# Squares and their seven block sums in one buffer, with one cast and one subtraction for the low parts

## The chip, the cores and the metric

The kernel runs on one core of one Trainium2 chip. The metric is the device time of one execution in microseconds (us); a run's number is the time of that one core. Five engines work in parallel, each through its own queue in order: TensorE (PE in the profile, its weight loads PEld), VectorE (DVE), ScalarE (ACT), GpSimd (POOL), and SyncE (SP), which issues the DMA transfers.

## What is computed

Two layers, of which the second stage takes nearly all of the matmuls. First a local attention (4 batches, 8 heads, 768 positions, head size 64): each position looks at keys less than 16 away and at one summary key for each block of 32. Its output `x` (3072 tokens, 512 wide) goes through a feed-forward layer with a squared ReLU:

```python
h = np.maximum(x @ w_in, 0.0)          # w_in  512 x 2048
return (h * h @ w_out)                 # w_out 2048 x 512
```

All products are made in float32 precision from two parts of each operand: a high part, rounded by a cast to `float32r`, and a low part, the rest. A product is high x high + high x low + low x high, so three matmuls.

## The kernel before

The 3072 tokens make 12 chunks of 256 (two tiles of 128). Chunks 0 and 1 and the preparation of the weights run in a start phase from a hand-written list of steps (`START`). From chunk 2 on, `period(c)` and `slot(c, n, ...)` write the program: a chunk has 8 slots, and slot n treats one pair p of blocks of 128 hidden units (256 hidden units in all). Every engine executes its instructions in the order in which the program writes them (the scheduler is off: `tc.manual_schedule`), so the order of the calls in `slot` is the order on each queue. A slot writes, in this order:

- the first layer of the pair: `ffn1_pair`, 24 matmuls of 256 columns (L392), into PSUM bank 4 or 5 (`ph`, alternating);
- in slot 7 the attention outputs of the next chunk's two tiles (`outputs`, L361), which read the transposed weights `pT`;
- the second layer of the pair of the slot before: `second`; in slots 0 and 3 also the scores of the next chunk's two tiles (L277);
- the lists `before`, the squares of this slot, `mid`, the rest of the squares, `after` and `last`. In them lies the next chunk's attention: maxima (`mask_max`, L304), exponentials (L312), sums' inverses (`inverse`, L322, L325), the norm on GpSimd (`norm`, L330), the 32x32 transposes (`turn`, L343), and the block sums of keys and values (L195, L200).

The second layer has two forms. The plain form (`second`, L586) is 12 matmuls of 512 columns. The other (`products`, L522) multiplies 2x2 blocks with seven block products instead of eight: 21 matmuls of 256 columns. It needs three sums of blocks of `w_out` (made once for each pair by `build(p, step)`: four steps on GpSimd, the fifth with casts on ScalarE, L499 and L500, and subtractions on VectorE, L501 and L502) and four sums of blocks of the squares, made in every slot. Before, chunks 0 to 2 are plain; from chunk 3 on all pairs but pair 0 use `products`. `BUILDS` says in which slot, and in which of the four lists (b, m, a, l), a step of a build stands: pairs 1 to 4 in chunk 2, the end of pair 4 and pairs 5, 7 and 6 in chunk 3. The sums of pairs 1, 3, 5 and 7 are stored to DRAM and loaded again in every chunk (`stream`).

The squares of a slot with `products`, before (`squares_and_sums`, `split_sums`): ScalarE makes `r` = ReLU (L400) and from `r` the high parts of three of the four blocks by Square (L406). VectorE overwrites `r` with the squares (L440) and makes the four sums in a second buffer `s`: two by one 256-wide subtraction (L443), two 128 wide (L448, L449). GpSimd subtracts the low parts of the three blocks, 384 wide (L447). After the list `mid`, ScalarE casts the sums (L453) and GpSimd subtracts their low parts, 512 wide (L454). A plain slot (`squares`) has ReLU and Square on ScalarE and the square and the low parts on VectorE (L411, L414).

Pieces that a sentence can't say:

```python
passes = [(m, n) for m in plain for n in range(3)] + [(m, n) for m in summed for n in range(2)]
for (blk, b, n_ps, o), n in passes + [(m, 2) for m in summed]:
    g_, w = ((gh_sb, 0), (gh_sb, 1), (gl_sb, 0))[n]      # n = 2 reads the low parts gl
```

The functions that the change touches, and what calls them:

Of the kernel before, what the change touches and what calls it, by code (L numbers as in the profile page):

```python
# [864 lines left out]
```

## Time and profile before

| | us |
|---|---|
| runs (three): median, lowest, highest | 667.4, 666.64, 669.68 |
| the profiled execution's own time | 667.81 |
| span of its profile | 666.0 |
| PE busy | 609.5 (92%), 5859 matmuls |
| VectorE (DVE) busy | 510.1 (77%) |
| ScalarE (ACT) busy | 291.6 (44%) |
| GpSimd (POOL) busy | 277.9 (42%) |
| chain that ended last, by engine | PE 39%, DVE 38%, ACT 12%, issue 5%, POOL 4%, DMA 1% |

The time of an execution and the span of its profile differ by what lies before the first and after the last instruction (1.8 us here). PE's busy time counts pipelined matmuls with modelled ends, so 92% does not say that PE has no time to lose. The start phase takes the span up to about 140 us, chunk 2 up to about 203 us, and chunks 3 to 11 the rest. In the views, an idle time in brackets, as `[2.15 <-DVE pT L343]`, stands behind the instruction that waited and names what came last; the line is that of the instruction that it waited for.

### The profile page before, as it was taken

Reading aid. Unit: us, or ns where it says so; the run is one execution under the profiler, and the core shown is the slowest. Engines: PE = TensorE matmul, PEld = TensorE weight load, DVE = VectorE, ACT = ScalarE, POOL = GpSimd, SP = SyncE. Lnnn points to the kernel's source line nnn. Section 1 sums busy time; section 2 is a strip of 40 time slices with the busy share of each in tenths; the row PEclk is TensorE's granted clock in tenths of the full one; section 3 lists DMA queues with packets and bytes.
Section 4 is the critical chain, followed back from the end, with each engine's and each line's share of the span. In section 5 each row is a group of like instructions: output and inputs, shape, how many; then the busy total and the mean of one; then the engine's idle time right before and its main releaser. Section 6 shows DMA issues by size and latency. Waiting matters only on the chain.

```text
span 666.0 us, 14839 instructions
## 1 busy us (share of the span) xinstructions
PE 609.5 (92%) x5859; PEld 567.6 (85%) x5859; DVE 510.1 (77%) x1240; ACT 291.6 (44%) x748; POOL 277.9 (42%) x252
## 2 busy tenths in 40 slices
PE   3689999999989788998999998998998999999997
PEld 2578888988878788998988998988998998998897
DVE  4898998957756876787787788788698588588554
ACT  3678685224444333443443443443434444443232
POOL 3635462005637662442453343343254244244242
PEclk9789999999989977999999999998999999999999
DMA  8689311550216421732621732732532432331410
GB/s 337 215 351 376 116 64 48 184 189 1 88 58 200 171 96 65 237 111 96 215 88 48 238 112 96 230 120 74 186 104 83 138 132 82 127 97 48 155 67 33
DMA packets 27638, 91.15 MB, mean 137 GB/s; under 512 B 3376, under 2 KB 3504, under 8 KB 25520
## 3 DMA queue, kind: packets, MB, share of 16 engines
q1 hardware_dynamic: 27568, 90.20, 39.2%
q8 instruction: 46, 0.75, 0.5%
q14 instruction: 24, 0.20, 0.1%
HBM read 80.75 MB, written 9.44 MB: 135 GB/s over the span
## 4 chain that ended last, share of the span: by engine, by line
PE 39%; DVE 38%; ACT 12%; issue 5%; POOL 4%; DMA 1%; DVEq 0%; SPq 0%; ACTq 0%; POOLq 0%
PE ph L392 17%; DVE pT L343 8%; DVE s L443 8%; PE zw L522 6%; ACT e_sb L312 5%; DVE r L440 4%; PE o_ps L463 4%; PE o_ps L522 4%; PE o_ps L586 3%; ACT r L400 2%; DVE s L448 2%; DVE s L449 2%; ACT gh L406 2%; DVE e_sb L304 2%; DVE w_sb L263 1%
## 5 line engine op out<-in xcount | busy, mean ns | idle before, releaser
L392 PE MATMUL ph<-xh,w_sb 128*128 128x256 f32 x1408 | 251.9, 281 | 2.0 <-DVE gl L414 1.1
L392 PEld LDWEIGHTS ph<-xh,w_sb 128*128 128x128 f32 x1408 | 215.9, 189 | 8.2 <-issue 2.7
L392 PE MATMUL ph<-xl,w_sb 128*128 128x256 f32 x704 | 197.1, 280 | 0.2
L392 PEld LDWEIGHTS ph<-xl,w_sb 128*128 128x128 f32 x704 | 132.8, 189 | 1.6 <-DVE xl L377 1.6
L447 POOL TENSOR_TENSOR gl<-r,gh 128x384 fp32r<-128x384 f32 x63 | 64.5, 1024 | 150.4 <-DVE r L440 145.7
L453 ACT CAST gh<-s 128x512 fp32r<-128x512 f32 x63 | 39.1, 621 | 181.2 <-DVE s L449 171.6
L454 POOL TENSOR_TENSOR gl<-s,gh 128x512 fp32r<-128x512 f32 x63 | 81.9, 1300 | 76.2 <-issue 58.4
L343 DVE STREAM_TRANSPOSE pT<-e_sb 32x256 f32<-32x256 f32 x228 | 99.4, 436 | 3.3
L400 ACT ACTIVATE r<-ph 128x512 f32<-128x512 f32 x85 | 50.3, 592 | 84.1 <-PE ph L392 36.7
L312 ACT ACTIVATE e_sb<-e_sb,nmx 128x120 f32<-128x120 f32 x192 | 73.5, 384 | 25.9 <-DVE nmx L304 25.9
L330 POOL TENSOR_TENSOR e_sb<-e_sb,sm 128x480 f32<-128x480 f32 x43 | 43.3, 1008 | 96.2 <-DVE sm L325 88.6
L443 DVE TENSOR_TENSOR s<-r 128x256 f32<-128x256 f32 x63 | 75.4, 1197 | 6.5
L440 DVE TENSOR_TENSOR r<-ph,r 128x512 f32<-128x512 f32 x63 | 43.5, 691 | 37.5 <-ACT gh L406 30.3
L406 ACT ACTIVATE gh<-r 128x384 fp32r<-128x384 f32 (+1 forms) x96 | 54.0, 562 | 20.5 <-PE o_ps L463 12.9
L522 PE MATMUL zw<-sums,gh 128*128 128x256 f32 x252 | 51.5, 286 | 0.7 <-ACT gh L453 0.6
L522 PE MATMUL zw<-w_sb,gh 128*128 128x256 f32 x252 | 51.7, 287 | 0.3 <-ACT gh L406 0.3
L522 PE MATMUL o_ps<-w_sb,gh 128*128 128x256 f32 x252 | 50.3, 281 | 0.0
L256 POOL TENSOR_TENSOR w_raw<-w_raw 128x1024 int32<-128x1024 int32 x16 | 34.2, 2147 | 37.0 <-DVE w_raw L251 13.9
L304 DVE CUSTOM_DVE_ANT_0 e_sb<-s_ps,mask_sb 128x120 f32<-128x120 f32 x192 | 42.6, 274 | 8.2 <-PE s_ps L292 5.8
L586 PE MATMUL o_ps<-w_sb,gh 128*128 128x512 f32 x144 | 46.1, 402 | 0.2 <-ACT gh L406 0.2
L411 DVE TENSOR_TENSOR ph<-ph,r 128x512 f32<-128x512 f32 x25 | 17.4, 695 | 33.6 <-ACT r L400 33.3
L522 PEld LDWEIGHTS zw<-sums,gh 128*128 128x128 f32 x252 | 39.5, 194 | 2.0 <-ACT gh L453 2.0
(119 smaller groups left out, 1165.4 us busy)
## 6 DMA issues: line engine op xcount, KB each, us to landing
sums<-sums SPq DMA_DIRECT2D x40, 768.0 KB, 4.8
w_raw<-in_w SPq DMA_DIRECT2D x16, 1024.0 KB, 10.2
v_sb<-in_v SPq DMA_DIRECT2D x24, 384.0 KB, 6.7
k_sb<-in_k SPq DMA_DIRECT2D x18, 384.0 KB, 5.4
q_sb<-in_q SPq DMA_DIRECT2D x24, 256.0 KB, 5.5
out<-ob SPq DMA_DIRECT2D x22, 256.0 KB, 2.1
kv<-in_kt SPq DMA_DIRECT2D x8, 384.0 KB, 3.2
kv_sb<-in_kt SPq DMA_DIRECT2D x8, 384.0 KB, 4.0
```

The costliest lines, as they stand in the source:

```text
L304: nc.vector.tensor_tensor_reduce(out=e_sb[:, h, 0:NK], in0=s_ps[g][h % 2][:, h // 2, 0:NK], in1=m, scale=-scale, scalar=3.0e38, op0=ALU.ad ...
L312: nc.scalar.activation(e, e, AF.Exp, bias=nmx[half][:, i : i + 1], scale=-1.0, accum_out=sm[half][:, i : i + 1])
L343: nc.vector.transpose(out=pT[g % 2][j * 32 : j * 32 + 32, :, i * 32 : i * 32 + 32], in_=e_sb[i * 32 : i * 32 + 32, :, j * 32 : j * 32 + 32],)
L392: nc.tensor.matmul(ph, lhsT=w_sb[f][:, w, cc * P : (cc + 1) * P], rhs=x[c][:, cc, :], start=(n == 0), stop=(n == 3 * NC4 - 1))
L400: nc.scalar.activation(r, ph, AF.Relu)
L406: nc.scalar.activation(gh, r, AF.Square)
L440: nc.vector.tensor_mul(out=r, in0=ph, in1=r)
L443: nc.vector.tensor_sub(out=s_sb[:, 0 : 2 * P].rearrange("p (a b) -> p a b", a=2), in0=a21.unsqueeze(1).to_broadcast([P, 2, P]), in1=r[:, P ...
L447: nc.gpsimd.tensor_sub(out=gl_sb[:, k, o], in0=r[:, o], in1=gh_sb[:, k, o].bitcast(F32))
L454: nc.gpsimd.tensor_sub(out=gl_sb[:, k, o], in0=s_sb, in1=gh_sb[:, k, o].bitcast(F32))
L522: nc.tensor.matmul(bank[n_ps][:, o], lhsT=g_[:, k, blk * P : (blk + 1) * P], rhs=b[:, w], start=False, stop=(n == 2 and (n_ps, o.start) in ...
L586: nc.tensor.matmul((X, Y)[tt], lhsT=g_[tt], rhs=w_sb[2 * p + i][:, w, DM:], start=(begins and i == 0 and m == 0), stop=(ends and i == 1 an ...
```

## The change

- `squares_and_sums` writes the squares and their sums into one buffer of seven blocks (`r_sb`, 896 wide); ReLU goes into its own buffer `h_sb` and Square is gone. After `mid`, `split` casts all seven blocks at once on ScalarE and subtracts all low parts at once on GpSimd. In a plain slot `split` does the same with four blocks, 512 wide; VectorE keeps only the square.
- `products` does the high parts of all seven blocks first and then seven matmuls with low parts.
- `BUILDS` is written by a rule: pairs 1, 2, 3 in chunk 2, pairs 5 and 7 in chunk 3, pairs 4 and 6 in chunk 4. `PRODUCTS_FROM` says from which chunk a pair uses `products`: 1, 2, 3, 5, 7 from chunk 3, 4 and 6 from chunk 4. So pairs 4 and 6 of chunk 3 are plain.
- The small buffers `nmx` are 6 instead of 7, and the scratch for DMA descriptors is 512 bytes instead of 1024.

```diff
@@ -36,14 +36,14 @@
 FROM_KT = 6
 NP = NF // 2
 STREAMED = (1, 3, 5, 7)
+PRODUCTS_FROM = {1: 3, 2: 3, 3: 3, 5: 3, 7: 3, 4: 4, 6: 4}
 BUILDS = {
-    2: [(2, "a", 1, 0), (2, "a", 1, 1), (3, "b", 1, 2), (3, "b", 1, 3), (3, "a", 1, 4)]
-    + [(4, "b", 2, 0), (4, "b", 2, 1), (4, "a", 2, 2), (4, "a", 2, 3), (5, "b", 2, 4)]
-    + [(5, "a", 3, 0), (5, "a", 3, 1), (6, "b", 3, 2), (6, "b", 3, 3), (6, "a", 3, 4)]
-    + [(7, "b", 4, 0), (7, "b", 4, 1), (7, "a", 4, 2), (7, "a", 4, 3)],
-    3: [(0, "b", 4, 4), (0, "a", 5, 0), (0, "a", 5, 1), (0, "a", 5, 2), (0, "a", 5, 3), (1, "a", 5, 4)]
-    + [(2, "b", 7, 0), (2, "b", 7, 1), (3, "b", 7, 2), (3, "b", 7, 3), (3, "a", 7, 4)]
-    + [(4, "b", 6, 0), (4, "b", 6, 1), (5, "b", 6, 2), (5, "b", 6, 3), (5, "a", 6, 4)],
+    c: [(n, "a", p, step) for p, at in pairs for step, n in enumerate(at)] + [(at[3] + 1, "b", p, 4) for p, at in pairs]
+    for c, pairs in {
+        2: ((1, (1, 1, 2, 2)), (2, (3, 3, 4, 4)), (3, (5, 5, 6, 6))),
+        3: ((5, (1, 2, 2, 3)), (7, (4, 4, 5, 5))),
+        4: ((4, (1, 2, 2, 3)), (6, (4, 4, 5, 5))),
+    }.items()
 }
 LAST_ORDER = (2, 1, 4, 3, 6, 5, 7, 0)
 MASKED = -1.0e9
@@ -102,8 +102,8 @@
     pT = [const.tile([P, H, P], F32, name=f"pT{i}") for i in range(2)]
     ksums = [const.tile([P, NPAIR, NB], F32, name=f"ksum{i}") for i in range(2)]
     vsum = const.tile([P, NPAIR, 32], F32, name="vsum")
-    r_sb = const.tile([P, DM], F32, name="r")
-    s_sb = const.tile([P, DM], F32, name="s")
+    h_sb = const.tile([P, DM], F32, name="h")
+    r_sb = const.tile([P, 7 * P], F32, name="r")
     gh_sb = const.tile([P, 2, 7 * P], F32R, name="gh")
     gl_sb = const.tile([P, 2, 7 * P], F32R, name="gl")
     xh_sb = const.tile([P, NPAIR, CT], F32R, name="xh")
@@ -427,31 +427,27 @@
 
     def squares(ph, k):
 
-        r = relu(ph, r_sb, nc.scalar)
-        high_square(flat(gh_sb, k), r)
-        square(ph, r)
-        low_square(flat(gl_sb, k), ph, flat(gh_sb, k))
+        h = relu(ph, h_sb, nc.scalar)
+        nc.vector.tensor_mul(out=r_sb[:, 0:DM], in0=ph, in1=h)
+        return lambda: split(k, DM)
 
     def squares_and_sums(ph, k):
 
-        r = relu(ph, r_sb, nc.scalar)
-        o = slice(0, 3 * P)
-        high_square(gh_sb[:, k, o], r[:, o])
-        nc.vector.tensor_mul(out=r, in0=ph, in1=r)
-        a12, a22, a11, a21 = (r[:, i * P : (i + 1) * P] for i in range(4))
-        s1, s3, s2, s4 = (s_sb[:, i * P : (i + 1) * P] for i in range(4))
-        nc.vector.tensor_sub(
-            out=s_sb[:, 0 : 2 * P].rearrange("p (a b) -> p a b", a=2), in0=a21.unsqueeze(1).to_broadcast([P, 2, P]),
-            in1=r[:, P : 3 * P].rearrange("p (a b) -> p a b", a=2),
+        h = relu(ph, h_sb, nc.scalar)
+        r = r_sb.rearrange("p (a b) -> p a b", b=P)
+        nc.vector.tensor_mul(
+            out=r_sb[:, 0 : 6 * P].rearrange("p (a b) -> p a b", a=2)[:, :, 0:CT],
+            in0=ph.rearrange("p (a b) -> p a b", a=2), in1=h.rearrange("p (a b) -> p a b", a=2),
         )
-        nc.gpsimd.tensor_sub(out=gl_sb[:, k, o], in0=r[:, o], in1=gh_sb[:, k, o].bitcast(F32))
-        nc.vector.tensor_sub(out=s2, in0=a11, in1=s1)
-        nc.vector.tensor_sub(out=s4, in0=a12, in1=s2)
-
-    def split_sums(k):
-        o = slice(3 * P, 7 * P)
-        nc.scalar.copy(out=gh_sb[:, k, o], in_=s_sb)
-        nc.gpsimd.tensor_sub(out=gl_sb[:, k, o], in0=s_sb, in1=gh_sb[:, k, o].bitcast(F32))
+        nc.vector.tensor_sub(out=r[:, 2:5:2], in0=r[:, 4:5].to_broadcast([P, 2, P]), in1=r[:, 1:4:2])
+        nc.vector.tensor_sub(out=r[:, 5], in0=r[:, 3], in1=r[:, 2])
+        nc.vector.tensor_sub(out=r[:, 6], in0=r[:, 0], in1=r[:, 5])
+        return lambda: split(k, 7 * P)
+
+    def split(k, n):
+        gh = gh_sb[:, k, 0:n]
+        nc.scalar.copy(out=gh, in_=r_sb[:, 0:n])
+        nc.gpsimd.tensor_sub(out=gl_sb[:, k, 0:n], in0=r_sb[:, 0:n], in1=gh.bitcast(F32))
 
     X, Y, Z, W = bank[6], bank[7], bank[2], bank[3]
 
@@ -514,10 +509,10 @@
         t3, t4, t2 = (sums[p][:, :, i * CT : (i + 1) * CT] for i in range(3))
         t1, b11, b21, b22 = halves(2 * p, 1), halves(2 * p, 0), halves(2 * p + 1, 0), halves(2 * p + 1, 1)
         lo, hi = slice(0, CT), slice(CT, DM)
-        plain = (2, b11, 2, lo), (0, b21, 6, lo), (1, t4, 7, lo)
-        summed = (4, t3, 3, lo), (3, t1, 3, hi), (5, t2, 2, hi), (6, b22, 6, hi)
-        passes = [(m, n) for m in plain for n in range(3)] + [(m, n) for m in summed for n in range(2)]
-        for (blk, b, n_ps, o), n in passes + [(m, 2) for m in summed]:
+        plain = (3, b11, 2, lo), (0, b21, 6, lo), (1, t4, 7, lo)
+        summed = (4, t3, 3, lo), (2, t1, 3, hi), (5, t2, 2, hi), (6, b22, 6, hi)
+        passes = [(m, n) for ms in (plain, summed) for m in ms for n in range(2)]
+        for (blk, b, n_ps, o), n in passes + [(m, 2) for m in plain + summed]:
             g_, w = ((gh_sb, 0), (gh_sb, 1), (gl_sb, 0))[n]
             nc.tensor.matmul(
                 bank[n_ps][:, o], lhsT=g_[:, k, blk * P : (blk + 1) * P], rhs=b[:, w],
@@ -569,15 +564,20 @@
     def order(c):
         return LAST_ORDER if c == n_c - 1 else range(NP)
 
+    def in_products(c, p):
+        return c >= PRODUCTS_FROM.get(p, n_c)
+
     def second(c, n):
 
         p, k = order(c)[n], n % 2
         begins, ends = n == 0, n == NP - 1
-        summed = c > 2
-        if summed and begins:
+        if begins and c > 2:
             open_banks(*((Z, W) if p == 0 else (X, Y, Z, W)))
-        if p in built:
-            products(p, k, ((2, CT), (3, CT), (6, CT), (7, 0)) if ends else ((2, CT), (3, CT)) if n == NP - 2 and c == n_c - 1 else ())
+        if in_products(c, p):
+            closes = ((6, CT), (7, 0)) if ends else ()
+            if not any(in_products(c, later) for later in list(order(c))[n + 1 :]):
+                closes += ((2, CT), (3, CT))
+            products(p, k, closes)
             return
         for tt in range(TPC):
             for i in range(2):
@@ -604,8 +604,7 @@
             scores(a + 1, 0, NPAIR)
         for do in before:
             do()
-        summed = c > 2 and p > 0
-        (squares_and_sums if summed else squares)(ph, k)
+        rest = (squares_and_sums if in_products(c, p) else squares)(ph, k)
         if n == NP - 1 and a < n_g:
             for g in (a, a + 1):
                 high_x(g)
@@ -618,8 +617,7 @@
                 evict(c - 1, NF - 1, tt, nc.scalar)
         for do in mid:
             do()
-        if summed:
-            split_sums(k)
+        rest()
         for do in after:
             do()
         for do in last:
```

Where instructions stand before and after, at the places that the prediction speaks of. The first is VectorE's queue in slot 1 of a chunk from 4 on (`r` and `s` are the buffers of squares and sums, `sm` the sums of the exponentials). Before:

```order
L440 TENSOR_TENSOR r<-ph,r 128x512
L443 TENSOR_TENSOR s<-r 128x256
L448 TENSOR_TENSOR s<-r,s 128x128
L449 TENSOR_TENSOR s<-r,s 128x128
L322 SCALAR_TENSOR_TENSOR sm<-sm 128x4
```

After:

```order
L438 TENSOR_TENSOR r<-ph,h 128x2x256
L442 TENSOR_TENSOR r<-r 128x2x128
L443 TENSOR_TENSOR r<-r 128x128
L444 TENSOR_TENSOR r<-r 128x128
L322 SCALAR_TENSOR_TENSOR sm<-sm 128x4
```

VectorE's own queue keeps its order; the sums stay in the buffer of the squares.

The second is GpSimd's queue in chunk 4, from slot 1 (`e_sb` are the exponentials that a norm scales, `ob` the buffer in which weights' sums are built). Before, to the start of slot 3:

```order
L447 TENSOR_TENSOR gl_84<-r_81,gh_83 128x384
L330 TENSOR_TENSOR e_sb_75<-e_sb_75,sm_2775 128x4x120
L454 TENSOR_TENSOR gl_84<-s_82,gh_83 128x512
L330 TENSOR_TENSOR e_sb_75<-e_sb_75,sm_2799 128x4x120
L447 TENSOR_TENSOR gl_84<-r_81,gh_83 128x384
L454 TENSOR_TENSOR gl_84<-s_82,gh_83 128x512
L447 TENSOR_TENSOR gl_84<-r_81,gh_83 128x384
```

After, slots 1 to 3:

```order
L330 TENSOR_TENSOR e_sb_75<-e_sb_75,sm_2715 128x4x120
L450 TENSOR_TENSOR gl_84<-r_82,gh_83 128x896
L483 TENSOR_TENSOR ob_87<-w_sb_930 128x512
L330 TENSOR_TENSOR e_sb_75<-e_sb_75,sm_2738 128x4x120
L450 TENSOR_TENSOR gl_84<-r_82,gh_83 128x896
L483 TENSOR_TENSOR ob_87<-w_sb_999 128x512
L486 TENSOR_TENSOR ob_87<-ob_87 128x256
L487 TENSOR_TENSOR ob_87<-ob_87 128x256
L450 TENSOR_TENSOR gl_84<-r_82,gh_83 128x896
L490 TENSOR_TENSOR ob_87<-ob_87 128x256
L491 TENSOR_TENSOR ob_87<-ob_87 128x256
```

The norm now stands ahead of a slot's only low-part subtraction, and the build of pair 4 lies between the slots' subtractions, where chunk 4 had no build.

The third is ScalarE's queue in chunk 4 from the cast of slot 3 to that of slot 4. Before:

```order
L453 CAST gh_83<-s_82 128x512
L400 ACTIVATE r_81<-ph_100 128x512
L406 ACTIVATE gh_83<-r_81 128x384
L312 ACTIVATE e_sb_75,sm_3000<-e_sb_75,nmx_2999 128x120 x4
L453 CAST gh_83<-s_82 128x512
```

After:

```order
L449 CAST gh_83<-r_82 128x896
L495 CAST sums_2939<-ob_87 128x768
L496 CAST w_sb_930<-ob_87 128x256
L400 ACTIVATE h_81<-ph_100 128x512
L312 ACTIVATE e_sb_75,sm_2945<-e_sb_75,nmx_2944 128x120 x4
L449 CAST gh_83<-r_82 128x896
```

The two casts of the build now stand ahead of slot 4's ReLU, and Square is gone from between ReLU and exponentials.

## Rows read from the trace of the kernel before

**Rows 1.** Windows, chunks 3, 4, 7, 10: length, busy PE PEld DVE ACT POOL, clock

```profile
202.98:266.72 63.74, 54.36 (x483) 50.91 (x482) 49.09 (x107) 24.24 (x66) 35.46 (x35) 0.89 0.37 130
266.72:318.92 52.20, 48.89 (x484) 46.30 (x482) 42.35 (x109) 21.18 (x60) 19.99 (x18) 1.00 0.42 142
...
421.25:474.20 52.95, 49.69 (x483) 47.38 (x482) 42.34 (x109) 21.18 (x60) 19.97 (x18) 0.97 0.41 140
...
574.61:625.04 50.43, 47.79 (x453) 45.48 (x452) 39.84 (x103) 22.17 (x61) 22.29 (x20) 1.00 0.28 91
```

**Rows 2.** Timeline of PE, chunk 7, slots 2 and 3: start, duration, engine, line

```profile
424.48 0.41 PE L392 MATMUL ph<-xh,w_sb 128*128 128x256 f32 x2
...
427.22 0.39 PE L522 MATMUL zw<-w_sb,gh 128*128 128x256 f32 x2
...
429.61 0.40 PE L392 MATMUL ph<-xh,w_sb 128*128 128x256 f32 x2
...
435.36 1.05 PE L277 MATMUL s_ps<-k_sb,q_sb 64*64 64x120 f32 x32
```

**Rows 3.** Waits, whole span: who waited for whom, us in total, times, longest

```profile
PE s_ps L361 <- DVE pT L343: 14.8, 9, 2.7
...
PEld zw L522 <- POOL gl L454: 7.9, 17, 1.0
```

**Rows 4.** Timeline of PE, chunk 7, slot 7

```profile
460.42 0.69 PE L361 MATMUL s_ps<-pT,v_sb 128*64 128x64 f32 x16 [2.15 <-DVE pT L343]
```

**Rows 5.** Timeline of VectorE, chunk 7, slots 4 to 7

```profile
442.39 0.69 DVE L440 TENSOR_TENSOR r<-ph,r 128x512 f32<-128x512 f32 x1
443.18 1.27 DVE L443 TENSOR_TENSOR s<-r 128x256 f32<-128x256 f32 x1
444.48 0.29 DVE L448 TENSOR_TENSOR s<-r,s 128x128 f32<-128x128 f32 x1
...
447.31 0.46 DVE L322 SCALAR_TENSOR_TENSOR sm<-sm 128x4 f32<-128x4 f32 x1 [1.14 <-ACT e_sb L312]
...
448.40 0.69 DVE L440 TENSOR_TENSOR r<-ph,r 128x512 f32<-128x512 f32 x1 [0.42 <-ACT gh L406]
...
455.84 0.69 DVE L440 TENSOR_TENSOR r<-ph,r 128x512 f32<-128x512 f32 x1
...
460.40 0.69 DVE L440 TENSOR_TENSOR r<-ph,r 128x512 f32<-128x512 f32 x1
```

**Rows 6.** Timeline of GpSimd, chunk 7, slot 4

```profile
443.15 1.02 POOL L447 TENSOR_TENSOR gl<-r,gh 128x384 fp32r<-128x384 f32 x1 [2.22 <-DVE r L440]
...
446.47 1.27 POOL L454 TENSOR_TENSOR gl<-s,gh 128x512 fp32r<-128x512 f32 x1
```

**Rows 7.** Line L443, whole span: duration ns minimum, median, maximum, first and last start

```profile
L443 DVE TENSOR_TENSOR s<-r x63: 425/1268/1278, 205.1 to 654.2; 128x256 f32<-128x256 f32 x63
```

**Rows 8.** Groups by line and shape, whole span: busy us, mean ns, idle before

```profile
L454 POOL TENSOR_TENSOR gl<-s,gh 128x512 fp32r<-128x512 f32 x63 | 81.9, 1300 | 76.2 <-issue 58.4 <-ACT gh L453 17.8
...
L330 POOL TENSOR_TENSOR e_sb<-e_sb,sm 128x480 f32<-128x480 f32 x43 | 43.3, 1008 | 96.2 <-DVE sm L325 88.6 <-ACT r L400 7.2 <-ACT gh L406 0.4
...
L453 ACT CAST gh<-s 128x512 fp32r<-128x512 f32 x63 | 39.1, 621 | 181.2 <-DVE s L449 171.6 <-DVE sm L322 9.6
...
L406 ACT ACTIVATE gh<-r 128x384 fp32r<-128x384 f32 x63 | 33.1, 525 | 2.0
...
L414 DVE TENSOR_TENSOR gl<-ph,gh 128x512 fp32r<-128x512 f32 x25 | 17.3, 690 | 2.4 <-ACT gh L406 0.4
...
L137 ACT CAST w_sb<-w_raw 128x1024 fp32r<-128x1024 f32 x8 | 9.1, 1135 | 4.3 <-DVE w_sb L263 4.3
...
L263 POOL TENSOR_TENSOR w_sb<-w_raw,w_sb 128x1024 fp32r<-128x1024 f32 x3 | 7.6, 2535 | 2.4 <-ACT w_sb L137 2.3
...
L499 ACT CAST sums<-ob 128x768 fp32r<-128x768 f32 x7 | 5.8, 833 | 12.1 <-POOL ob L495 12.1
...
L490 POOL TENSOR_TENSOR ob<-ob 128x256 f32<-128x256 f32 x7 | 5.2, 742 | 0.1
```

More of the change, by code (lines that the diff above doesn't have):

```diff
@@ L301, in mask_max @@
         if half not in nmx:
-            nmx[half] = work.tile([P, 4], F32, name="nmx", tag="nmx", bufs=7)
+            nmx[half] = work.tile([P, 4], F32, name="nmx", tag="nmx", bufs=6)
             sm[half] = work.tile([P, 4], F32, name="sm", tag="sm", bufs=7)
@@ L470, in operands @@
         return [[g_[:, k, b * P : (b + 1) * P] for b in FIRST[i]] for g_ in (gh_sb, gl_sb)]
-    built, sums = set(), {}
+    sums = {}
     dram = {p: tc.dram_tile([P, 1536], F32, name=f"sums{p}") for p in STREAMED}
@@ L504, in build @@
             nc.sync.dma_start(out=dram[p].rearrange("p (h c) -> p h c", h=2), in_=t.bitcast(F32))
-        built.add(p)
     def stream(p, tag_room=True):
@@ L633, in period @@
             steps["bmal".index(where)][n].append(lambda p=p, step=step: build(p, step))
-        if c > 2:
-            last[0].append(lambda: stream(1))
-            last[2].append(lambda: stream(3))
-            last[4].append(lambda: stream(5))
-            if c < n_c - 1:
-                last[6].append(lambda: stream(7))
-            else:
-                last[1].append(lambda: stream(7, False))
+        for p in STREAMED:
+            if in_products(c, p):
+                if c == n_c - 1 and p == 7:
+                    last[1].append(lambda: stream(7, False))
+                else:
+                    last[p - 1].append(lambda p=p: stream(p))
         a = 2 * c + 2
@@ L763, in begin @@
         elif op == "RE":
-            r_of[i] = relu(ph_of[i], r_sb, eng)
+            r_of[i] = relu(ph_of[i], h_sb, eng)
         elif op == "SQ":
@@ L854 @@
     arrays["mean"] = _mean()
-    nc = bacc.Bacc("TRN2", target_bir_lowering=False, num_devices=1, dynamic_dma_scratch_size=1024)
+    nc = bacc.Bacc("TRN2", target_bir_lowering=False, num_devices=1, dynamic_dma_scratch_size=512)
     args = [
```

## The prediction

> **What bounds the kernel now.** First the busy table by chunk [rows 1]; a chunk's stretch runs from the opening of banks Z and W in its slot 1 to the next such opening. Chunks 5 to 10 lie between 318.92 and 625.04: 306.1 us, 51.0 each. To see what TensorE alone would need, read its starts in the timeline [rows 2]: a pair's first layer starts at 424.48, its products at 427.22, the next pair at 429.61, so 2.74 us for 24 matmuls and 2.39 for 21. The opening and the plain pair 0 take the 3.23 from the end of the stretch before, 421.25, to 424.48. A chunk has eight first layers (21.9), seven product slots (16.7), 3.2 for pair 0, two score groups of 1.0 (the row at 435.36) and 64 attention-output matmuls, about 2.4 (four times the 16 at 460.42 [rows 4]): 46.2. So some 5 us a chunk are lost.
>
> Next, who is waited for [rows 3]: TensorE for VectorE's transposes (14.8 us, nine waits, one a chunk, 2.15 in chunk 7 [rows 4]), and for GpSimd's low parts of the sums (7.9). Then VectorE's own timeline in chunk 7 [rows 5] beside GpSimd's [rows 6]. VectorE's 256-wide subtraction starts at 443.18 and takes 1.27 us; GpSimd's low-part subtraction began at 443.15 and takes 1.02. The same subtraction has a minimum of 0.425 and a median of 1.268 over its 63 runs [rows 7]. At 447.31 a VectorE instruction four elements wide takes 0.46 and ends 0.03 after GpSimd's 446.47 + 1.27. I read this as: a VectorE instruction with two SBUF inputs that meets a running GpSimd one waits until that is over. VectorE's in-order queue then brings the transposes late. That is the bound in chunks 5 to 10; in chunk 3 (63.74 us, clock 0.89) the building of the weights' sums comes on top.
>
> **The change, part by part.** *Low parts moved behind the sums.* The 384-wide GpSimd subtraction no longer starts with VectorE's: 1.27 becomes 0.43, 0.84 saved in each of 63 slots, 5.9 us of VectorE a chunk. In the plain slot one 0.69 subtraction leaves VectorE too [rows 8].
>
> *Square gone from ScalarE's front.* VectorE's product starts after the ReLU instead of after Square: 0.53 earlier [rows 8]. At 448.40 VectorE did wait 0.42 for just this [rows 5].
>
> *One cast, 896 wide.* Between 0.833 (768) and 1.135 (1024): I take 0.98, against 0.62 for the 512 of before [rows 8]. Bounds 0.84 and 1.14.
>
> *One GpSimd subtraction, 896 wide.* 1.30 for 512, 2.54 for 1024 with the same output type: by the line between them 2.23; bounds 2.05 and 2.32 (the two old ones, 1.01 + 1.30, together) [rows 8]. [...]
>
> *Later deadlines do not cover all.* From the start of the product, the low parts were done after 0.80 + 1.27 + 0.33 + 0.32 + 0.09 + 0.62 + 0.08 + 1.30 = 4.81; now after 0.80 + 0.46 + 0.33 + 0.32 + 0.09 + 0.98 + 0.08 + 2.23 = 5.29. (0.80 is product and hand-over, 442.39 to 443.18; 0.33 the spacing of the 128-wide ones [rows 5].) They are wanted 14 matmuls into the products, 1.6 us, instead of 17, 1.9. That is 0.8 tighter, but the product starts 0.53 earlier and VectorE has 0.84 less in each slot before. Slots 1 to 5 keep margins of some 0.4 to 0.9, and I cost them at nothing. If that cover goes, each tenth past it costs up to 6 us over 63 slots.
>
> *The one buffer.* The product of the next slot must wait until cast and subtraction have read the buffer, 5.3 after the last product. Slots are 5.1 to 6 apart except 6 to 7, where before they were 455.84 and 460.40, 4.56 [rows 5]. There the product of slot 7 now waits; behind it in VectorE's queue stand its three subtractions and the two halves of the next chunk's x, 3.1 us, and TensorE waits for those. So the wait for transposes goes and one for x of about 1.5 us comes.
>
> *Laid out.* With these durations I worked the queues out in program order, each instruction starting when its engine is free and its inputs are there, hand-overs of 0.08 to 0.22, and VectorE and GpSimd shutting each other out as above. The kernel before so gives 299.7 for chunks 5 to 10 (traced 306.1), 60.3 for chunk 3 (63.7) and 51.2 for chunk 4 (52.2); what is short is clock and small gaps. The kernel after gives 282.7: **-17.0**.
>
> *Sums over three chunks: chunk 4.* It had no builds and gets two, behind 2.23-long low parts. From the opening: GpSimd does slot 1's low parts to 6.4, a 512-wide add (1.3, as its 512-wide subtraction) to 7.7, a norm (1.0) to 8.7; slot 2's low parts 10.6 to 12.8, an add to 14.1, two 256-wide ones (0.74) to 16.6 with VectorE's subtractions between; slot 3's low parts to 18.8, two adds to 20.3 (each duration from [rows 8]). Only then come the build's casts, which stand ahead of slot 4's ReLU on ScalarE, and its subtractions ahead of the product on VectorE: product at 23.3, high parts at 26.1. TensorE wanted them at 22.6 and waits 3.5, then 1.0 for the low parts. The second build delays slot 6 alike (3.4 and 1.9 before the outputs). Chunk 4 comes to 58.9 where it was 51.2: **+7.7**.
>
> *Chunk 3* has two builds instead of a good three and two plain slots (2.8 instead of 2.4 on TensorE): 54.9 for 60.3, **-5.4**. *Chunk 2* builds three pairs instead of four, but its low parts now queue on GpSimd with them, 1.30 each instead of VectorE's 0.69 (waits of 0.9 to 2.4): **+1.9**. *The end:* the last pair's low parts wait for product, cast and 1.30 with only 2.4 us of products as cover: **+0.9**. [...]
>
> *At nothing:* six `nmx` buffers for seven (a chunk uses four in turn, and each is free once its norm is done) and the smaller DMA scratch (the loads go out on SP); the stores and loads of the sums of 5 and 7 in chunk 3 have two slots, about 10 us, and cost under 1 each if they miss.
>
> *Clock.* Chunk 7 is 1.9 longer than the mean of 51.0, at a clock of 0.97 [rows 1], after its 2.15 wait: that wait goes, -1. Chunk 4 gets waits over 3 us, and after such waits chunk 3's clock was 0.89 [rows 1]: +1.5.
>
> Sum: -17.0 + 7.7 - 5.4 + 1.9 + 0.9 - 1 + 1.5 = -11.4. The profiled execution took 667.81, its span 666.0; 667.8 - 11.4 = **656**. The median of the runs, 667.4, is 0.4 below it.
>
> **Rivals.** *Low parts become the bound of every slot (slower).* Place: the wait of TensorE before the last seven matmuls. The chain from product to low parts is laid at 5.29; it decides from about 0.55 longer on (all margins eaten, some 5 us for each further tenth): 0.25 longer gives back 6, 0.5 gives back 16, 0.75 gives 28, so 684. For it: GpSimd also does a norm in slots 1, 2, 4 and 5, and VectorE's small instructions may now wait 2.2 instead of 1.3. Against: 384, 512 and 1024 wide lie close to a line. *No change.* Half of that, or chunks 3 and 4 as long as chunk 3 was (63.7, +5 and +9 more): 666 to 668. *Builds cost less.* If each costs the 3 us on the path that chunk 3's did (60.3 less 51, over three), chunk 4 loses 5 of its 7.7, chunk 3 as much: 648. *It doesn't do what it says:* if VectorE's subtraction still meets GpSimd (a norm or the low parts of the slot before), its row stays near 1.27 and the time near 672.
>
> **How the numbers follow.** Forecast as laid out 0.62, builds cheaper 0.12: both faster. No change 0.11. Low parts as the bound, or the lock in another place, 0.15. A difference under 0.5% (3.3 us) cannot be told from none here. So faster 0.74, same 0.11, slower 0.15. The bounds of cast and subtraction alone move the sum from 650 to 661; with cheap builds it goes to 645, and upwards I take in no change and the first part of the slower cases, to 671.
>
> **What would show it.** Right: VectorE's first subtraction near 0.43; the wait for transposes nearly gone, one for x instead; chunks 5 to 10 at 47 to 48 each; chunk 4 longer than before, with waits on casts and low parts; a GpSimd subtraction of 2.2 us. Wrong: waits for low parts in most slots of chunks 5 to 10, or chunk 4 no longer than 52.

## The result, and the profile after

| | us |
|---|---|
| before: median of the runs on the same chip (4 runs) | 668.1 |
| changed kernel: median, lowest, highest (4 runs) | 645.56, 644.92, 646.46 |
| ratio, with its 95% interval | 0.966, 0.964 to 0.969 |
| span of the changed kernel's profile (before: 666.0) | 644.0 |

The forecast was 656, faster. The time lies inside the range of 645 to 671, but at its lower edge, and the gain is twice the one in the sum: 22 us instead of 11.4.

The windows of the changed kernel by chunk (length, busy time of PE, PEld, DVE, ACT, POOL, then the clock), for chunks 3, 4, 5, 7 and 10, answer to [rows 1]:

```profile
203.24:258.94 55.70, 51.09 (x466) 47.42 (x464) 39.10 (x98) 21.34 (x57) 29.48 (x24) 0.94 0.44 147
258.94:318.09 59.15, 52.29 (x483) 50.07 (x482) 42.53 (x112) 22.09 (x57) 31.18 (x24) 0.91 0.37 125
318.09:365.26 47.17, 47.17 (x484) 45.65 (x482) 35.03 (x108) 20.04 (x53) 21.74 (x15) 1.00 0.37 124
...
413.14:461.00 47.86, 47.43 (x483) 45.68 (x482) 36.58 (x108) 20.13 (x53) 20.00 (x12) 1.00 0.47 155
...
555.08:602.15 47.07, 46.53 (x454) 45.13 (x453) 34.39 (x103) 20.51 (x52) 20.83 (x12) 1.00 0.30 98
```

In chunk 5 PE is busy for the whole stretch, and VectorE's busy time is 5 to 6 us below what [rows 1] show for chunks 7 and 10. Chunk 4 has become the longest.

The changed kernel's lines of the squares, by line (duration in ns, minimum/median/maximum), which answer to [rows 7], and by group and shape, which answer to [rows 8]:

```profile
L438 DVE TENSOR_TENSOR r<-ph,h x61: 673/692/694, 204.2 to 629.7; 128x512 f32<-128x512 f32 x61
L442 DVE TENSOR_TENSOR r<-r x61: 424/426/1108, 204.9 to 630.4; 128x256 f32<-128x256 f32 x61
```

```profile
L450 POOL TENSOR_TENSOR gl<-r,gh 128x896 fp32r<-128x896 f32 x61 | 129.4, 2121 | 129.2 <-ACT gh L449 123.5 <-issue 5.8
L449 ACT CAST gh<-r 128x896 fp32r<-128x896 f32 x61 | 57.6, 944 | 115.7 <-DVE r L444 108.3 <-DVE sm L322 7.4
```

VectorE's first subtraction has its own 0.43 us again. GpSimd's long subtraction takes 2.12 and the cast 0.94, both a little under the estimates.

TensorE's waits in chunks 5 to 10 before (us in total, times, longest):

```profile
PE s_ps L361 <- DVE pT L343: 8.1, 6, 2.1
PE zw L522 <- POOL gl L454: 3.0, 6, 0.8
...
PEld zw L522 <- POOL gl L454: 6.0, 13, 1.0
```

and in the same chunks of the changed kernel:

```profile
PE ph L392 <- DVE xl L377: 0.8, 2, 0.4
PE o_ps L526 <- DVE ob L555: 0.5, 1, 0.5
...
PEld zw L517 <- POOL gl L450: 0.3, 2, 0.2
```

The waits for transposes are gone, and those for low parts with them. These waits are not the whole gain. Chunks 5 to 10 as one window, before:

```profile
318.92:625.04 306.12, 292.18 (x2858) 277.25 (x2857) 243.57 (x635) 127.62 (x361) 126.09 (x116) 0.99 0.37 121
```

In the changed kernel the same window has 284.06 and a busy time of 282.64. So TensorE's idle time fell by 12.5 us, and 9.5 more came off its busy time with the same matmuls, 6.7 of them in the products (L522 116.34, L517 109.69, 882 matmuls each). No line of the waits shows these 9.5; what they were made of is not shown.

### The profile page after: what moved, and what is told of

It reads as the page before. It is cut to its first block, busy times and chain, and to the rows that moved or that the text cites. A ratio compares the mean times of both kernels' runs of the same rounds, so it can differ in the third digit from the quotient of the medians.

```text
span 644.0 us, 14622 instructions
## 1 busy us (share of the span) xinstructions
PE 601.3 (93%) x5841; PEld 563.8 (88%) x5841; DVE 456.1 (71%) x1217; ACT 280.1 (43%) x685; POOL 286.1 (44%) x206
## 4 chain that ended last, share of the span: by engine, by line
PE 62%; DVE 14%; POOL 8%; ACT 6%; issue 5%; DMA 3%; SPq 0%; POOLq 0%; DVEq 0%; ACTq 0%
PE ph L392 28%; PE zw L517 9%; PE o_ps L517 7%; PE o_ps L586 6%; POOL gl L450 4%; PE o_ps L459 4%; ACT e_sb L312 3%; PE s_ps L277 2%; DVE pT L343 2%; DMA v_sb<-in_v 2%; DVE r L438 1%; POOL e_sb L330 1%; ACT gh L449 1%; DVE sm L322 1%; DVE r L442 1%
## 5 line engine op out<-in xcount | busy, mean ns | idle before, releaser
L450 POOL TENSOR_TENSOR gl<-r,gh 128x896 fp32r<-128x896 f32 (+1 forms) x80 | 153.9, 1923 | 217.9 <-ACT gh L449 212.1
L449 ACT CAST gh<-r 128x896 fp32r<-128x896 f32 (+1 forms) x80 | 69.3, 866 | 128.6 <-DVE r L444 108.3
L400 ACT ACTIVATE h<-ph 128x512 f32<-128x512 f32 x85 | 50.8, 598 | 114.0 <-PE ph L392 110.4
L438 DVE TENSOR_TENSOR r<-ph,h 128x512 f32<-128x512 f32 x61 | 42.1, 690 | 48.1 <-ACT h L400 36.5
L586 PE MATMUL o_ps<-w_sb,gh 128*128 128x512 f32 x160 | 53.1, 415 | 3.8 <-ACT gh L449 3.8
L517 PE MATMUL zw<-w_sb,gh 128*128 128x256 f32 x244 | 49.4, 284 | 3.3 <-ACT gh L449 3.3
L517 PE MATMUL o_ps<-w_sb,gh 128*128 128x256 f32 x244 | 48.4, 280 | 0.0
L517 PE MATMUL zw<-sums,gh 128*128 128x256 f32 x244 | 48.3, 280 | 0.0
L517 PEld LDWEIGHTS zw<-w_sb,gh 128*128 128x128 f32 x244 | 37.6, 191 | 4.0 <-ACT gh L449 3.5
L322 DVE SCALAR_TENSOR_TENSOR sm<-sm 128x4 f32<-128x4 f32 x48 | 21.6, 449 | 27.4 <-ACT e_sb L312 27.4
L586 PEld LDWEIGHTS o_ps<-w_sb,gh 128*128 128x128 f32 x160 | 30.8, 198 | 10.6 <-ACT gh L449 4.4
L431 DVE TENSOR_TENSOR r<-ph,h 128x512 f32<-128x512 f32 x19 | 13.1, 688 | 34.9 <-ACT h L400 34.8
L459 PE MATMUL o_ps<-w_sb,gh 128*128 128x512 f32 x120 | 37.5, 394 | 0.0
```

The lines of the kernel that those rows point to most:

```text
L400: nc.scalar.activation(r, ph, AF.Relu)
L438: nc.vector.tensor_mul(out=r_sb[:, 0 : 6 * P].rearrange("p (a b) -> p a b", a=2)[:, :, 0:CT], in0=ph.rearrange("p (a b) -> p a b", a=2), i ...
L449: nc.scalar.copy(out=gh, in_=r_sb[:, 0:n])
L450: nc.gpsimd.tensor_sub(out=gl_sb[:, k, 0:n], in0=r_sb[:, 0:n], in1=gh.bitcast(F32))
L459: nc.tensor.matmul((X, Y)[tt], lhsT=g_[tt], rhs=w_sb[f][:, w, DM:], start=(first and n == 0), stop=(last and n == 2),)
L517: nc.tensor.matmul(bank[n_ps][:, o], lhsT=g_[:, k, blk * P : (blk + 1) * P], rhs=b[:, w], start=False, stop=(n == 2 and (n_ps, o.start) in ...
```

## The experiments

Theory: GpSimd's low-part subtraction beside VectorE's sums held VectorE up, and its place behind the sums is the gain. Rivals: Square's removal is the gain, or the plan of the builds is. All the edits were timed beside the kernel before on the same chip; a ratio is to that kernel's runs (medians from 667.06 to 668.21). Where an edit is set beside the changed kernel's 645.6, the two may come from different chips; the kernel before differed by up to 1.2 us between them.

### The two halves of the change

*The changed kernel with the builds of before* (`BUILDS` as the kernel before has it):

```diff
-PRODUCTS_FROM = {1: 3, 2: 3, 3: 3, 5: 3, 7: 3, 4: 4, 6: 4}
+PRODUCTS_FROM = {p: 3 for p in range(1, 8)}
```

> The changed kernel with the builds of the kernel before: pairs 1 to 4 in chunk 2, the end of 4 and 5, 7 and 6 in chunk 3, all seven pairs with products from chunk 3 on. Theory (the squares' part is the gain, the plan about neutral): laid out, chunk 4 gives back its 11 us, chunk 3 takes 7 more, chunk 2 takes 2.7 more, which makes 644; with a lower clock in chunk 3, as before the change, up to 649. Rival 2 (the plan of the builds is the gain, since over 10 us of it were not in the sum): 656 or above.

Measured: 646.0 (ratio 0.967, 0.966 to 0.969).

*The kernel before with the new builds* (squares, sums, low parts and order of the products as before):

```diff
+PRODUCTS_FROM = {1: 3, 2: 3, 3: 3, 5: 3, 7: 3, 4: 4, 6: 4}
...
+        2: ((1, (1, 1, 2, 2)), (2, (3, 3, 4, 4)), (3, (5, 5, 6, 6))),
+        3: ((5, (1, 2, 2, 3)), (7, (4, 4, 5, 5))),
+        4: ((4, (1, 2, 2, 3)), (6, (4, 4, 5, 5))),
```

> The kernel before with only the new plan of the builds, and its chunk 3 pairs 4 and 6 in the plain form; squares, sums, low parts and the order of the products as before. Theory (the plan is about neutral): laid out +1.3, so 665 to 671, chunk 4 near 58 to 60, chunk 3 near 56 to 58, chunks 5 to 10 at 51. Rival 2 (the plan is the gain): 655 or below.

Measured: 663.2 (0.994, 0.992 to 0.996), below the expected 665 to 671. So 667.7 before, 663.2 with the plan alone, 646.0 with the squares' part alone, 645.6 with both. The squares' part is the gain. The plan gives 4.5 with the old squares and nothing to speak of with the new ones. Its chunks 3 and 4 with the old squares:

```profile
198.01:254.68 56.67, 50.38 (x465) 46.83 (x464) 42.10 (x101) 22.73 (x62) 27.11 (x26) 0.97 0.43 145
254.68:314.21 59.53, 51.69 (x484) 48.71 (x482) 47.16 (x113) 23.41 (x64) 31.70 (x30) 0.94 0.38 125
```

With the old builds the new squares' chunks 3 and 4 are:

```profile
208.32:271.02 62.70, 51.78 (x484) 49.11 (x483) 47.25 (x106) 22.70 (x59) 35.22 (x30) 0.95 0.38 131
271.02:318.89 47.87, 47.44 (x484) 45.69 (x482) 36.59 (x108) 20.11 (x53) 19.97 (x12) 1.00 0.47 155
```

Chunk 4 without builds is as short as the later ones; the two builds in it cost 11 us, which the plan saves again in chunk 3 (62.70 to 55.70) and before chunk 3 (its start goes from 208.32 to 203.24). With the old squares it saves as much there (63.74 to 56.67, start from 202.98 to 198.01), but its builds cost only 7.3 in chunk 4 (52.20 to 59.53). That is where the 4.5 goes: chunk 4 with two builds takes 59 us with either squares, so the new squares gain hardly anything there.

### The meeting of the two engines

*GpSimd beside the sums again*:

```diff
+        o = slice(0, 3 * P)
+        nc.gpsimd.tensor_sub(out=h[:, o], in0=h[:, o], in1=h[:, o])
         nc.vector.tensor_sub(out=r[:, 2:5:2], in0=r[:, 4:5].to_broadcast([P, 2, P]), in1=r[:, 1:4:2])
```

> The changed kernel with one GpSimd subtraction more in each slot with products: 384 wide, started when VectorE's product is done, on the buffer of the ReLU, which nobody reads any more; the result is not used. GpSimd so runs again beside VectorE's sums, and nothing else is changed. Theory (the gain comes from VectorE no longer meeting GpSimd): VectorE's first subtraction goes from a median of 0.43 back to about 1.27 us and more than the whole gain is lost, since the low parts, now all behind it, come 0.84 later too: laid out with the same durations +32, so 670 to 678. Rival 1 (the gain comes from the product's start 0.5 us earlier, without Square): GpSimd has over half of each slot free, so 646 to 651. Rival 2 (the gain is the plan of the builds): the same, 646 to 651.

Measured: 665.0 (0.996, 0.995 to 0.998): 19.5 of the 22 us are gone. That is the theory's direction and not the rivals' (646 to 651), though below the 670 to 678 expected. One detail did not come as expected. VectorE in chunk 7 (L444 to L446 are the three subtractions here):

```profile
436.10 0.42 DVE L444 TENSOR_TENSOR r<-r 128x256 f32<-128x256 f32 x1
436.56 0.80 DVE L445 TENSOR_TENSOR r<-r 128x128 f32<-128x128 f32 x1
437.39 0.29 DVE L446 TENSOR_TENSOR r<-r 128x128 f32<-128x128 f32 x1
```

and GpSimd beside it:

```profile
436.14 1.07 POOL L443 TENSOR_TENSOR h<-h 128x384 f32<-128x384 f32 x1 [1.11 <-DVE r L438]
```

The second subtraction over all its slots:

```profile
L445 DVE TENSOR_TENSOR r<-r x61: 699/799/1279, 205.4 to 651.0; 128x128 f32<-128x128 f32 x61
```

GpSimd came 0.04 after VectorE's first subtraction, which then ran undisturbed; the second one met it and took 0.80 instead of 0.29, until 437.36, 0.15 after GpSimd's end. So the loss was 0.51 a slot and not 0.84: here VectorE's subtraction that started ahead of GpSimd's took its 0.42, and the one that started while GpSimd's ran took 0.80. GpSimd's subtraction started while VectorE's first one had 0.38 to go, and took 1.07 instead of 1.02 [rows 6]. VectorE's product, whose other input is PSUM, keeps 692 ns at a maximum of 694 in the changed kernel (first fence of L438 above).

*The same GpSimd work, after the sums*: it reads the last of the sums, so that it cannot start earlier.

```diff
         nc.vector.tensor_sub(out=r[:, 6], in0=r[:, 0], in1=r[:, 5])
+        o = slice(0, 3 * P)
+        nc.gpsimd.tensor_sub(out=h[:, o], in0=h[:, o], in1=r_sb[:, 4 * P : 7 * P])
```

> As the first experiment, the changed kernel with the same useless 384-wide GpSimd subtraction in each slot with products, at the same place in GpSimd's queue, but it reads the last of VectorE's sums, so that it starts when they are done, during ScalarE's cast. GpSimd's load is that of the first experiment, VectorE's sums are not met, and the low parts start about 0.1 us later than without it. Theory (the meeting of the engines costs the time): chunks 5 to 10 laid out at 288, expected 286 to 291 in place of 284, and the whole 650 to 658, most of it in chunks 3 and 4, where the builds want GpSimd. Rival (the load of GpSimd, not the meeting, made the first experiment slow): chunks 5 to 10 near 299 again and the whole near 665.

Measured: 653.2 (0.980, 0.978 to 0.983), as expected. Chunks 5 to 10 as one window, in the changed kernel, with the work after the sums, and with it beside them:

```profile
318.09:602.15 284.06, 282.64 (x2859) 273.34 (x2858) 210.57 (x630) 120.67 (x317) 124.32 (x78) 1.00 0.39 130
```

```profile
319.19:609.15 289.96, 286.46 (x2858) 274.58 (x2857) 220.46 (x630) 120.40 (x317) 166.24 (x121) 1.00 0.39 127
```

```profile
321.91:621.13 299.22, 291.63 (x2858) 277.30 (x2857) 233.67 (x630) 119.84 (x317) 168.69 (x121) 1.00 0.38 123
```

The load on GpSimd is the same in the last two (166 and 169 us busy). Behind the sums it costs 5.9, beside them 9.3 more. The 5.9 is not load alone: the added work now meets VectorE's four-element sums of L322, which stand right behind the sums in its queue and take 0.62 in the mean over the whole span instead of 0.45.

*The kernel before without the meeting*:

```diff
-        nc.gpsimd.tensor_sub(out=gl_sb[:, k, o], in0=r[:, o], in1=gh_sb[:, k, o].bitcast(F32))
```

> The kernel before with one instruction left out: GpSimd's 384-wide subtraction that makes the low parts of three blocks in a slot with products (the products there read what an earlier plain slot left in the buffer, so the output is not the reference's). Square stays, the product still waits for it, the builds and the order of the products stay. Theory (GpSimd beside VectorE's sums is the cause in the kernel before): VectorE's first subtraction falls from a median of 1.27 to about 0.43, TensorE's 14.8 us of waits for transposes go, chunks 5 to 10 come to 46.5 to 48 each in place of 51.0, and the whole to 635 to 645. Rival (Square ahead of the product costs at least as much): chunks 5 to 10 stay above 49, the whole above 652.

Measured: 631.1 (0.946, 0.943 to 0.950), below the expected 635. Chunks 5 to 10, and VectorE's first subtraction:

```profile
305.77:588.04 282.27, 281.69 (x2858) 273.17 (x2857) 207.51 (x635) 129.42 (x361) 82.26 (x73) 1.00 0.39 131
```

```profile
L443 DVE TENSOR_TENSOR s<-r x63: 424/426/954, 203.6 to 616.8; 128x256 f32<-128x256 f32 x63
```

With Square in its old place the chunks come to 47.0, and TensorE has hardly a gap left (busy 281.7 of 282.3). So it was this one instruction that held the kernel before. The run also takes 1.0 of load a slot off GpSimd and a wait for three low parts off TensorE; how much of its 24 us in these chunks is the meeting alone it does not tell, the pair above does.

### The product's start and the order of the products

*The product 0.5 later*:

```diff
         h = relu(ph, h_sb, nc.scalar)
+        nc.scalar.activation(h[:, 0 : 3 * P], h[:, 0 : 3 * P], AF.Relu)
```

> The changed kernel with one ScalarE pass of 384 columns more between the ReLU and VectorE's product (a second ReLU in place, which changes nothing), so that the product starts about 0.5 us later, as with Square. Theory (freed VectorE is the gain): the margin of the low parts absorbs most, laid out +4.8 over chunks 3 to 11: 648 to 653, chunks 5 to 10 at 47.5 to 48.5. Rival 1 (the earlier product is the gain): half of the 22 us or more comes back, 657 or above.

Measured: 652.8 (0.977, 0.976 to 0.979); the added pass takes 0.525. So with the low parts behind the sums a product that starts as late as behind Square costs 7.2 us: a third of the gain, less than the rival wanted and at the top of what the theory allowed.

*The old order of the products*:

```diff
-        passes = [(m, n) for ms in (plain, summed) for m in ms for n in range(2)]
-        for (blk, b, n_ps, o), n in passes + [(m, 2) for m in plain + summed]:
+        passes = [(m, n) for m in plain for n in range(3)] + [(m, n) for m in summed for n in range(2)]
+        for (blk, b, n_ps, o), n in passes + [(m, 2) for m in summed]:
```

> The changed kernel with only the order of the products undone: the low part of each of the first three blocks right after its two high parts, so that the first low part is wanted 2 matmuls into the products instead of 14, while all come from the one late subtraction. Theory (low parts last is needed, the margin is a few tenths of a us): TensorE waits for low parts in the first matmuls of some slots; laid out +6.4, chunks 5 to 10 at 48 to 49 each, 649 to 656. Rival (the low parts are there long before): 644 to 647.

Measured: 657.6 (0.985, 0.983 to 0.988): 12 of the 22 us gone, a little more than the theory's 649 to 656 allowed. The waits of PEld in chunks 5 to 10:

```profile
PEld zw L517 <- POOL gl L450: 8.6, 20, 0.9
```

Against 0.3 in the changed kernel: low parts made this late are covered here only because they are wanted last.

### The builds

*The end of a build later in its slot* (step 4 in list a, behind the slot's cast, instead of b):

```diff
-    c: [(n, "a", p, step) for p, at in pairs for step, n in enumerate(at)] + [(at[3] + 1, "b", p, 4) for p, at in pairs]
+    c: [(at[3] + 1, "a", p, 4) for p, at in pairs] + [(n, "a", p, step) for p, at in pairs for step, n in enumerate(at)]
```

> The changed kernel with only the fifth step of each build (casts on ScalarE, subtractions on VectorE) moved in its slot: behind the slot's cast, no longer ahead of the slot's ReLU. GpSimd's queue stays as it is. Theory (chunks 2 to 4 lose their time because ScalarE and VectorE stop at the build's casts until GpSimd's fourth step is done, and the slot's squares stand behind them): laid out, chunk 3's opening comes 5 earlier, chunk 3 takes 51 to 52 in place of 55.7, chunk 4 56 to 57 in place of 59.2, so 632 to 638. Rival (GpSimd itself has too much to do in these chunks, wherever the end of a build stands): 644 to 648.

Measured: 637.9 (0.956, 0.954 to 0.957), at the upper end of what was expected. Chunk 3 opens at 197.62 (203.24 in the changed kernel) and takes 53.76, not 51 to 52; chunk 4 gains only 1.2 and takes 58.00, not 56 to 57, where VectorE's transposes are now waited for once, for 4.6. The trace of the changed kernel shows what the edit takes away. ScalarE in chunk 4, at the end of slot 3 and in slot 4:

```profile
274.80 0.95 ACT L449 CAST gh<-r 128x896 fp32r<-128x896 f32 x1 [3.82 <-DVE r L444]
279.51 0.83 ACT L495 CAST sums<-ob 128x768 fp32r<-128x768 f32 x1 [3.76 <-POOL ob L491]
280.25 0.40 ACT L496 CAST w_sb<-ob 128x256 fp32r<-128x256 f32 x1
280.56 0.59 ACT L400 ACTIVATE h<-ph 128x512 f32<-128x512 f32 x1
```

GpSimd in that stretch:

```profile
271.55 1.33 POOL L483 TENSOR_TENSOR ob<-w_sb 128x512 f32<-128x512 f32 x1
272.83 0.91 POOL L486 TENSOR_TENSOR ob<-ob 128x256 f32<-128x256 f32 x1
273.82 0.74 POOL L487 TENSOR_TENSOR ob<-ob 128x256 f32<-128x256 f32 x1
275.83 2.14 POOL L450 TENSOR_TENSOR gl<-r,gh 128x896 fp32r<-128x896 f32 x1 [1.26 <-ACT gh L449]
277.91 0.75 POOL L490 TENSOR_TENSOR ob<-ob 128x256 f32<-128x256 f32 x1
278.74 0.74 POOL L491 TENSOR_TENSOR ob<-ob 128x256 f32<-128x256 f32 x1
```

VectorE at slot 3's squares:

```profile
271.87 0.69 DVE L438 TENSOR_TENSOR r<-ph,h 128x512 f32<-128x512 f32 x1
272.60 0.56 DVE L442 TENSOR_TENSOR r<-r 128x256 f32<-128x256 f32 x1
273.19 0.70 DVE L443 TENSOR_TENSOR r<-r 128x128 f32<-128x128 f32 x1
273.93 0.79 DVE L444 TENSOR_TENSOR r<-r 128x128 f32<-128x128 f32 x1
```

and TensorE at the first products of slot 4's squares:

```profile
285.22 0.80 PE L517 MATMUL zw<-w_sb,gh 128*128 128x256 f32 x2 [3.31 <-ACT gh L449]
```

The build's casts wait 3.76 for GpSimd, the ReLU stands behind them, and TensorE waits 3.31 for slot 4's cast. The builds also bring the meeting back: slot 3's three subtractions take 0.56, 0.70 and 0.79 beside GpSimd's adds, 2.05 together instead of 1.01, while the product beside the same adds keeps 0.69.

*The plain slots as before* (Square on ScalarE, square and low parts on VectorE):

```diff
     def squares(ph, k):
         h = relu(ph, h_sb, nc.scalar)
-        nc.vector.tensor_mul(out=r_sb[:, 0:DM], in0=ph, in1=h)
-        return lambda: split(k, DM)
+        high_square(flat(gh_sb, k), h)
+        square(ph, h)
+        low_square(flat(gl_sb, k), ph, flat(gh_sb, k))
+        return lambda: None
```

> The changed kernel with the plain slots as before: Square on ScalarE for the high parts, the square in place and the low parts on VectorE; slots with products as changed. Theory (GpSimd's low parts in the plain slots of chunk 2 queue up behind the builds and took back what one build less gave there): chunk 2 about 5 us shorter, opening of chunk 3 at about 198 instead of 203.2, the rest within 1: 639 to 641. Rival (plain slots are covered wherever the low parts are made): 644 to 646.

Measured: 642.0 (0.963, 0.960 to 0.966), 1 us above what was expected. Chunk 3 opens at 198.28, 5.0 earlier, as expected; chunks 3 and 4 take 1.9 of it back. So GpSimd's low parts in the plain slots of chunk 2 cost 5, and they do so with either plan: chunk 3 opens 5.3 later with the new squares under the old builds (202.98 to 208.32), 5.2 later under the new ones (198.01 to 203.24). The edit before this one won the same 5 us in chunk 2 with the low parts left on GpSimd: there it is the build's casts standing ahead of a ReLU together with the longer GpSimd queue that costs, and either cure does.

*One build a chunk*, first alone, then with the plain slots on VectorE (the fifth number is the slot of the build's end):

```diff
+PRODUCTS_FROM = {1: 3, 2: 3, 3: 3, 5: 4, 7: 5, 4: 6, 6: 7}
...
-    c: [(n, "a", p, step) for p, at in pairs for step, n in enumerate(at)] + [(at[3] + 1, "b", p, 4) for p, at in pairs]
+    c: [(n, "a", p, step) for p, at in pairs for step, n in enumerate(at)]
...
+        3: ((5, (2, 3, 5, 6, 7)),),
+        4: ((7, (2, 3, 5, 6, 7)),),
+        5: ((4, (2, 3, 5, 6, 7)),),
+        6: ((6, (2, 3, 5, 6, 7)),),
```

> The changed kernel with its builds of pairs 5, 7, 4, 6 spread: one in each of the chunks 3, 4, 5, 6, the steps in slots 2, 3, 5, 6, 7 behind the low parts of the slot, and the pair with products from the chunk after. That makes eight plain slots more, 0.4 us each. Theory (in chunks 3 and 4 GpSimd is the engine waited for, two builds do not fit beside the low parts, one does): chunks 3 to 6 at 47 to 49 each instead of 55.7, 59.2, 47.2, 47.9: 622 to 630. Rival (a build costs its 5 us wherever it stands): 645 to 650, with the added plain slots.

Measured: 627.4 (0.941, 0.939 to 0.943). In this run and the next, the end of pair 7's build replaces a block of the weights one slot before its last plain use, so chunk 4's output is made with a sum in that block's place; the amount of work is the same.

> The two edits before together: one build a chunk from chunk 3 on, and the plain slots' low parts on VectorE. Theory: both gains add, 617 to 625, faster than both kernels. Rival (VectorE's plain low parts, 0.69 each, and its two-input subtraction meeting the builds on GpSimd cost as much as they save): the same as one build a chunk alone.

Measured: 622.8 (0.934, 0.932 to 0.937): both gains add.

*The same with pair 7 mended*:

```diff
-PRODUCTS_FROM = {1: 3, 2: 3, 3: 3, 5: 4, 7: 5, 4: 6, 6: 7}
+PRODUCTS_FROM = {1: 3, 2: 3, 3: 3, 5: 4, 7: 4, 4: 6, 6: 7}
...
-        4: ((7, (2, 3, 5, 6, 7)),),
+        4: ((7, (1, 2, 3, 5, 6)),),
```

> One build a chunk and plain slots on VectorE, with pair 7 mended: its build stands in slots 1, 2, 3, 5, 6 of chunk 4 and its products begin in chunk 4. (In the two runs of one build a chunk the end of pair 7's build replaced a block of the weights one slot before its last plain use, so that chunk 4's output was computed with a sum in the place of that block; the work was the same.) Expected: as there, 620 to 625. Rival (a build step in slot 1, where GpSimd has a norm, costs what it costs in the changed kernel): chunk 4 at 51 or more, 626 to 630.

Measured: 621.3 (0.931, 0.929 to 0.933), 24 us below the changed kernel. Its chunks 3 and 4:

```profile
198.50:246.72 48.22, 48.22 (x448) 44.68 (x447) 36.00 (x100) 19.80 (x55) 15.73 (x13) 1.00 0.37 125
246.72:294.26 47.54, 47.54 (x465) 45.14 (x464) 37.16 (x101) 20.96 (x55) 19.91 (x15) 1.00 0.49 168
```

PE is busy throughout, at a clock of 1.00: a build spread over a chunk costs nothing that can be seen there, where two in one chunk cost 8 to 12 us in the changed kernel. Not all of that is the spreading: this plan also puts the end of each build in chunks 3 to 6 behind the slot's cast, and that alone, with two builds a chunk, left chunks 3 and 4 at 53.76 and 58.00.

## Why the prediction was right, and where its size was wrong

| term | predicted | measured (spans) |
|---|---|---|
| chunks 5 to 10 | -17.0 | 284.06 - 306.12 = -22.1 |
| chunk 4 | +7.7 | 59.15 - 52.20 = +7.0 |
| chunk 3 | -5.4 | 55.70 - 63.74 = -8.0 |
| chunk 2 | +1.9 | 203.24 - 202.98 = +0.3 |
| end | +0.9 | 41.85 - 40.96 = +0.9 |
| clock, apart | +0.5 | in the rows above |
| sum | -11.4 | -22.0 |

**Right:** the bound and the cause. VectorE's first subtraction fell to 0.43, the waits for transposes went, chunks 5 to 10 stand at 47.3, chunk 4 became longer through the very casts that were named, and the runs show the meeting of GpSimd and VectorE as what held the kernel before.

**The step that failed** is the sentence that what the layout of the kernel before was short of "is clock and small gaps". That layout gave 299.7, 60.3 and 51.2 for chunks 5 to 10, 3 and 4; the trace had 306.1, 63.7 and 52.2, 10.8 more. By taking one layout from the other I assumed that these 10.8 would be there after the change too. They were not: the layout of the changed kernel gave 282.7, 54.9 and 58.9, and the trace has 284.1, 55.7 and 59.2, within 1.5%. In chunks 5 to 10 little of the 6.4 was clock: the granted clock was 0.97 in chunk 7 [rows 1], which is some 1.6 us of its 52.95 (an estimate from these two numbers), and 0.99 over all six. The rest was stalls of TensorE, and the change removed most of both. In chunk 3 the clock can be all of it: it rose from 0.89 to 0.94, worth some 3.7 by the same estimate, where the sum was short by 2.6. So the name for the 10.8 was partly right, and what failed was to count them as staying. The layout of the changed kernel set against the traced chunks of before would have given -23.4, -8.8 and +6.7, with chunk 2 and the end -22.7, and so 645.

That the time fell into the range is luck in part: the range reached down to 645 only by cheap builds, which chunk 4 did not have; the bounds of cast and subtraction alone ended at 650.

**Chunk 2** was mis-sized in two parts that nearly cancel: a build less was worth 5 (chunk 3's opening at 198.0 with the plan alone), GpSimd's low parts in plain slots cost 5.

**The buffer's wait** came (VectorE's product waited for GpSimd's subtraction eight times, 10.1 us in all), but the 1.5 us a chunk on TensorE behind it did not: its waits for x are 0.8 in all in chunks 5 to 10. This did not show in the total because TensorE's need was set low as well: 46.2 a chunk, where TensorE in the run of the kernel before without the meeting takes 47.0 with hardly a wait. Two errors cancel in part here, which is luck. Nor did chunk 4's wait of 1.0 for low parts come; its lower clock (0.91) cost more than the 1.5 in the sum, some 5.3 by the estimate above, and the traced chunk came out near the layout all the same.

**The rivals.** "Builds cost less" gave 648, the nearest number, for a wrong reason: chunk 4 cost what was laid out. (5 less in chunk 4 and as much in chunk 3 would be 646; the prediction's sum is 2 off.) "Low parts become the bound" is a real mechanism, with too high a price: 0.5 us more was to give back 16; the pass that took 0.525 gave back 7.2. "It doesn't do what it says" fell with the 0.43. The long subtraction took 2.12, below the line between its two rows (2.23) and within its bounds.

## What to carry to other kernels

Where a VectorE instruction takes three times its shortest duration, as the 256-wide subtraction did before (1.27 against 0.43), look at what GpSimd does at that moment; here moving the same GpSimd work behind the sums gave back 11.8 us (665.0 to 653.2), and leaving that work out 7.6 more, with what it makes consumed last. When a hand layout of the old kernel falls short of its trace, the missing time may be made of the very stalls that the change is about, as it was here in chunks 5 to 10: set the new layout against the traced time too. Work done once (builds) was best spread over a chunk here, and its end cost 7.7 us by standing ahead of the main chain's first instruction on an in-order queue.

## What was not expected of the hardware

The VectorE subtraction that started 0.04 us before GpSimd's kept its 0.42, so a shift that small changed which of VectorE's three subtractions paid, and how much: 0.51 instead of 0.84. And the first pair of matmuls after TensorE's wait of 3.31 took 0.80, the pairs behind it 0.63, where such pairs take 0.39 to 0.41 [rows 2]. The granted clock of that stretch is 0.50:

```profile
285.22:289.00 3.78, 3.78 (x17) 3.78 (x18) 2.25 (x6) 1.95 (x9) 3.78 (x4) 0.50 0.01 2
```

It was 1.00 up to 284, 0.71 from there to 285.22, still in the wait, and 0.50 to 291. Around chunk 4's other long wait, 3.06 to 301.72, it was 1.00 up to 301, 0.64 from 301 to 303 and 0.50 from 303 to 305. So behind both of chunk 4's long waits TensorE worked at about half the clock for some us (mean of the chunk 0.91, by the estimate above some 5.3 us on top of the waits). That the waits lowered it is read from this order alone.
